# A three-stage kernel in fp32 halves: the last pair's down product by seven products instead of eight

## The chip, the core and the metric

One core of a Trainium2 chip runs the whole program. The metric is the device time of one execution in microseconds, the median of several runs; lower is better. An engine's work is shown by the profiler in time from the first to the last instruction, which is called the span.

## The reference

Chunked attention feeds two feed-forward networks, all in float32, on 4608 tokens of width 512. What the change touches is the first network's last product (`w_out`) and the start of the second network.

```python
x = attention(q, k, v)                   # 8 x 576 tokens, chunks of 64, 8 heads of 64
rms = np.sqrt(np.mean(x * x, axis=-1, keepdims=True) + 1e-06)
xn = x / rms * rms_g
g = xn @ w_gate                          # 512 -> 1536
val = xn @ w_val                         # 512 -> 1536
x = (g / (1 + np.exp(-g)) * val) @ w_out # 1536 -> 512
h = x @ w_in                             # 512 -> 2048
out = (h * np.clip(h + 3.0, 0.0, 6.0) / 6.0) @ w_out2
```

## The kernel before

Tokens are worked in nine blocks of 512, features stand on the partitions. Each fp32 operand is kept as a high and a low half, and a product of two operands is three matmuls (high by high, low by high, high by low). Blocks 0 to 2 of the first network are done plainly. Blocks 3 to 8 are done in three pairs (`for p in range(3)`, L1366). In a pair, the up part (gate and value matrices) is done as a two-by-two block product by seven products (Strassen's method in Winograd's form): the sums of weight blocks (`wo` tiles, loaded from the scratch tensors `ops`) and the sums of token blocks (`xu` tiles) were made earlier, and `product` (L1003 to L1014) issues six matmuls for each of 14 slots. The down part (`w_out`) is not: for each of the two blocks and each of 12 feature groups `mm_down_a` (L1020 to L1031) issues 12 matmuls on weights `wd`, loaded from `keep_out`, and on activations split into halves `gs` by ScalarE and GpSimd (`split_wp`, L1357). `y_store` then moves the four banks out to `yd`.

The second network does block 0 plainly (L1522 to L1554, with `x_fill` beside it, which loads the next pair's activations `x4` from `yd` and makes its sums), and then four pairs in which both the up and the down part go by seven products; there `product_down` (L1584 to L1588) issues six matmuls per step on activation splits that `split_by` (L1578) makes on ScalarE and VectorE four steps ahead.

The order of work is written by hand: each engine executes what the Python code issues, in that order. Side work is placed by ticks: `at(t, fn)` puts a function in an agenda and `tick()` runs it, about every 12 matmuls. In the last pair the side work is `Stash`: it prepares the second network's weights, loads them on ScalarE's DMA queue and stores their sums from that queue. The weight loads (`wo`, `wd`, `wq`) and stores of results go on the SP queue in program order. Weight tiles come from a pool `wp` of 36 buffers of 4 KB per partition; the tiles `q k qT kT p v` of the attention are single buffers, used by the second network's weight loads (`Stream`) later. At the start, while the first tokens are attended, tiny matmuls named `warm0` to `warm3` keep TensorE busy; the digit names the tile whose PSUM bank they write (bank 2i + 1). They stand in the table `START`, an order written out by hand.

## Time and profile before

| what | value |
|---|---|
| median of 3 runs | 1654.99 us (1652.78 to 1657.39) |
| the profiled execution | 1653.22 us |
| its span | 1651.4 us |
| TensorE (PE) busy in the span | 1639.8 us, 99% |
| VectorE (DVE), ScalarE (ACT), GpSimd (POOL) busy | 1036.2, 846.2, 453.7 us |
| granted TensorE clock | 1.0 in every slice (2.4 GHz) |

The profile's page gives for each engine the time in which it executes something. The chain of waits follows, from the last instruction back, what released each step. The wait view lists who waited for whom; the windows view gives busy times in chosen stretches of the span; the timeline lists instructions in order of time. L with a number is a line of the program.

### The profile page before, as it was taken

How to read it: one execution, taken by the hardware profiler on the slowest of the kernel's cores; microseconds unless marked ns; L12 is line 12 of the kernel's file. 1: busy time of each engine (PE TensorE's matmuls, PEld its weight loads, DVE VectorE, ACT ScalarE, POOL GpSimd, SP SyncE). 2: the span in 40 equal slices, each digit the busy share in tenths (PEclk: the TensorE clock that was granted, in tenths of full speed). 3: DMA queues.
4: the chain of work that ended last, by engine and by line, in shares of the span. 5: the costliest groups of instructions: out<-in, count | busy, mean ns of one | idle time of the engine just before them, and what ended most of it. 6: DMA issues, size and time to landing. Idle time of an engine off the chain costs nothing.

```text
span 1651.4 us, 26427 instructions
## 1 busy us (share of the span) xinstructions
PE 1639.8 (99%) x9911; PEld 1348.9 (82%) x9911; DVE 1036.2 (63%) x1534; ACT 846.2 (51%) x1409; POOL 453.7 (27%) x331
## 2 busy tenths in 40 slices
PE   8999999999999999999999999999999999999998
PEld 7888887888888888888888878888888888888887
DVE  7997566655575755748334388358746764875475
ACT  6885445445464455645434344455545544654553
POOL 1002333322236422354226522140024003301310
PEclk9999999999999999999999999999999999999999
DMA  9924677747977698855979675767877796687666
GB/s 295 285 46 112 203 215 208 215 149 234 313 264 241 202 288 281 279 214 209 339 237 330 256 266 199 227 191 249 215 219 218 217 241 199 222 225 232 194 197 161
DMA packets 336097, 375.08 MB, mean 227 GB/s; under 512 B 184288, under 2 KB 260064, under 8 KB 335840
## 3 DMA queue, kind: packets, MB, share of 16 engines
q1 hardware_dynamic: 266080, 302.32, 59.8%
q10 hardware_dynamic: 69888, 71.06, 12.6%
q8 instruction: 79, 1.29, 0.3%
q14 instruction: 50, 0.41, 0.1%
HBM read 292.55 MB, written 80.74 MB: 226 GB/s over the span
## 4 chain that ended last, share of the span: by engine, by line
PE 95%; DVE 2%; DMA 1%; issue 1%; SPq 1%; POOL 0%; ACT 0%; DVEq 0%; POOLq 0%; ACTq 0%
PE PS L1014 39%; PE PS L1588 18%; PE PS L1003 13%; PE PS L1028 6%; PE PS L1029 6%; PE PS L1031 6%; PE PS L908 1%; PE PS L835 1%; DMA wo<-ops 1%; PE PS L817 1%; PE PS L1040 1%; PE PS L1036 1%; PE PS L1790 1%; PE PS L1037 1%; DMA x<-yd 0%
## 5 line engine op out<-in xcount | busy, mean ns | idle before, releaser
L1014 PE MATMUL PS<-xu,wo 128*128 128x512 f32 x1512 | 350.2, 391 | 0.5 <-DVE xu L1230 0.5
L1014 PEld LDWEIGHTS PS<-xu,wo 128*128 128x128 f32 x1512 | 282.0, 188 | 59.8 <-DVE xu L1230 0.9
L1014 PE MATMUL PS<-xo,wq 128*128 128x512 f32 x1344 | 305.3, 389 | 0.0
L1588 PE MATMUL PS<-gs,wq 128*128 128x512 f32 x1296 | 295.3, 389 | 0.0
L1014 PEld LDWEIGHTS PS<-xo,wq 128*128 128x128 f32 x1344 | 252.3, 188 | 52.3
L1588 PEld LDWEIGHTS PS<-gs,wq 128*128 128x128 f32 x1296 | 242.9, 188 | 51.8 <-DVE gs L1582 1.2
L1003 PE MATMUL PS<-XH,w 128*128 128x512 f32 x576 | 146.4, 395 | 1.0 <-DVE w L220 1.0
L1003 PEld LDWEIGHTS PS<-XH,w 128*128 128x128 f32 x576 | 106.2, 188 | 24.9 <-DVE w L220 1.8
L1028 PE MATMUL PS<-gs,wd 128*128 128x512 f32 x288 | 113.2, 393 | 0.0
L1029 PE MATMUL PS<-gs,wd 128*128 128x512 f32 x288 | 112.2, 389 | 0.0
L1059 POOL TENSOR_TENSOR al<-sg,ah 128x512 fp32r<-128x512 f32 x40 | 57.1, 1427 | 153.7 <-ACT ah L1057 152.5
L1360 POOL TENSOR_TENSOR gs<-gu,gs 128x512 fp32r<-128x512 f32 x60 | 84.1, 1421 | 45.7 <-ACT gs L1359 40.1
L1364 DVE TENSOR_TENSOR gu<-gu,PS 128x512 f32<-128x512 f32 x60 | 41.1, 686 | 86.5 <-ACT gu L1446 45.4
L1656 POOL TENSOR_TENSOR gt<-gx 128x512 f32<-128x512 f32 x8 | 10.4, 1294 | 296.5 <-DVE gx L1653 296.5
L1582 DVE TENSOR_TENSOR gs<-gu,gs 128x512 fp32r<-128x512 f32 x88 | 68.0, 792 | 31.7 <-ACT gs L1581 31.5
L1581 ACT CAST gs<-gt 128x512 fp32r<-128x512 f32 x96 | 58.3, 623 | 44.0 <-DVE gt L1725 33.0
L1519 DVE SCALAR_TENSOR_TENSOR gu<-gu,PS 128x512 f32<-128x512 f32 x48 | 32.8, 684 | 72.9 <-ACT gu L1516 72.9
L1003 PE MATMUL PS<-XL,w 128*128 128x512 f32 x288 | 77.3, 390 | 0.0
L1031 PE MATMUL PS<-gs,wd 128*128 128x512 f32 x288 | 77.0, 389 | 0.0
L1057 ACT CAST ah<-sg 128x512 fp32r<-128x512 f32 x52 | 32.4, 624 | 74.9 <-DVE sg L1344 48.5
L1581 ACT CAST gs<-gu 128x512 fp32r<-128x512 f32 x96 | 57.4, 620 | 25.0 <-DVE gs L1582 17.7
L1656 POOL TENSOR_TENSOR gt<-gu 128x512 f32<-128x512 f32 x24 | 32.6, 1359 | 129.0 <-DVE gu L1653 124.8
(249 smaller groups left out, 2833.3 us busy)
## 6 DMA issues: line engine op xcount, KB each, us to landing
wq<-stash_in SPq DMA_DIRECT2D x128, 512.0 KB
wo<-ops SPq DMA_DIRECT2D x126, 512.0 KB
wq<-sums_out SPq DMA_DIRECT2D x64, 512.0 KB
wq<-stash_out SPq DMA_DIRECT2D x48, 512.0 KB
wd<-keep_out SPq DMA_DIRECT2D x36, 512.0 KB
yd<-yst SPq DMA_DIRECT2D x18, 512.0 KB
ops<-w ACTq DMA_DIRECT2D x36, 256.0 KB
v<-in_v_dram SPq DMA_DIRECT2D x32, 256.0 KB
```

Source lines behind the costliest of these rows:

```text
L1003: nc.tensor.matmul(ps, w(wi, c), xs[c][xi], start=(i == 0), stop=(i == n - 1))
L1014: nc.tensor.matmul(PS[:, bank, :], op[:, wi, c * 128:(c + 1) * 128], x[xi][:, c, :], start=first and i == 0, stop=last and i == 5, skip_gr ...
L1028: nc.tensor.matmul(ps, wm[0], a[0], start=first, stop=False)
L1029: nc.tensor.matmul(ps, wm[1], a[0], start=False, stop=False)
L1031: nc.tensor.matmul(PS[:, banks[m], :], w[:, 0, m * 128:(m + 1) * 128], a[1], start=False, stop=last)
L1059: nc.gpsimd.tensor_tensor(lo, t, hi.bitcast(F32), op=ALU.subtract)
L1360: e.tensor_tensor(w[:, 1, :], t, w[:, 0, :].bitcast(F32), op=ALU.subtract)
L1364: nc.vector.tensor_tensor(o, x, y, op=op)
L1581: nc.scalar.copy(w[:, 0, :], x)
L1582: e.tensor_tensor(w[:, 1, :], x, w[:, 0, :].bitcast(F32), op=ALU.subtract)
L1588: nc.tensor.matmul(PS[:, banks[m], :], op[:, wi, m * 128:(m + 1) * 128], x[xi], start=first and (wi, xi) == (0, 0), stop=False, skip_group ...
L1656: nc.gpsimd.tensor_tensor(slot(i, "t"), slot(i, "12"), slot(i, "11"), op=ALU.subtract)
```

## The change

Three things are changed.

1. In the last pair (p == 2) the down part goes by seven products too, with `product_down` and `split_by` as in the second network. It has 42 steps of six matmuls (seven products, six feature groups each) in place of 24 groups of 12. The activations of the up part are laid out anew (`slot`): both token blocks and both features of a group go in tiles `1` and `2`, and GpSimd makes two differences per feature group (`sums_g`); a third is made on VectorE ahead of the step. The results go out as four halves (`kept`, `more`, `y_put`) at the ends of the seven groups of steps.
2. The sums of `w_out` blocks that this needs are made from the kept weights, in the last pair's up part: `OutSums`, six of them, five ticks apart, starting six ticks into the part. Each loads two `keep_out` tiles (SP queue), adds their halves, makes four sums and splits them again (VectorE and ScalarE), and stores four pieces to a new scratch tensor `keep_sums` from ScalarE's queue. Its tiles are the attention's buffers `q`, `k`, `kT`, `p`, used in turn. The down part loads 21 weight tiles (12 of sums, 9 of blocks, the latter in two DMAs each) in place of 12.
3. The second network's plain block uses other PSUM banks (2, 3 for its up product, 4 to 7 for its down product, before 6, 7 and 2 to 5), and asks for its first `x4` tile before its first product instead of after. In `START`, many `warm2` become `warm1`, `warm0` or `warm3`: their count and places stay, their banks change.

The diff, cut to its core (lines of `START` stand for the table; `split_by` and `product_down` are moved up unchanged):

```diff
-    out_q2 total3 total1 share3 share1 scores0 warm2 warm2 warm2 warm2 scores2 trans_p3 top0 less0 top2 less2 Wm0
-    out_p3 expo0 warm2 warm2 warm2 warm2 trans_p1 values3 out_p1 expo2 Wm1 out_x3 square3 total0 Wb0 total2 Wb1
+    out_q2 total3 total1 share3 share1 scores0 warm1 warm1 warm1 warm1 scores2 trans_p3 top0 less0 top2 less2 Wm0
+    out_p3 expo0 warm1 warm1 warm1 warm1 trans_p1 values3 out_p1 expo2 Wm1 out_x3 square3 total0 Wb0 total2 Wb1
...
+    class OutSums:
+        def buf(self, n, kind=F32):
+            return at_p.tile([128, 2, 512], kind, tag=(("q", "k"), ("kT", "p"))[self.i % 2][n], name="os")
...
+            for z, t in enumerate((self.u, self.r)):
+                nc.sync.dma_start(out=t, in_=o1[2 * self.i + z])
...
+            nc.vector.tensor_tensor(self.u[:, z, :], t[:, 0, :], t[:, 1, :], op=ALU.add)
...
+            tt(a22, a21, a22, op=ALU.add)
+            tt(a21, a11, a21, op=ALU.subtract)
+            tt(a11, a22, a11, op=ALU.subtract)
+            tt(a12, a12, a11, op=ALU.subtract)
...
+                nc.scalar.copy(self.h[:, z, :], u)
+                nc.vector.tensor_tensor(u.bitcast(F32R), u, self.h[:, z, :].bitcast(F32), op=ALU.subtract)
...
+                for y, t in enumerate((self.h.bitcast(F32), self.u)):
+                    nc.scalar.dma_start(
+                        out=e1[:, 2 * z:2 * z + 2, self.i, y, :],
...
+                (0, self.load), (4, self.whole, 0), (5, self.whole, 1), (6, self.sums), (7, self.split), (8, self.keep),
...
+        for k_, part in ((O11, 3), (O1, 3), (O2, 3), (O12, 2), (O3, 3), (O12, -1), (O4, 3), (O22, 3)):
+            order += [(2, "out", j, k_) for j in (range(part) if part > 0 else range(3 + part, 3))]
+        for i in range(NI):
+            OutSums(i).plan(P0 + 2 * PAIR + 6 + 5 * i)
...
+                    if p == 2 and i == NI - 1 and pr in (2, 7):
+                        nx.append(split_by(nc.gpsimd, slot(len(nx), "11")))
...
+                        if p == 2:
+                            sums_g(i_)
...
+            for n, (pr, i) in enumerate(steps):
...
+                product_down(bk[z], loads.t[key][:, i % 2], nx.popleft(), pr in (1, 5) and i == 0)
...
+                feed(n + 4)
...
-                for _ in range(1 + 5 * c):
+                for _ in range(6 if c else 2 if b == 1 else 1):
...
+        go(fill, 1)
...
-            bank = 6 + n % 2
+            bank = 2 + n % 2
...
-                mm_down_b(W["out2", fs[n - 1]], prev, n == 1, False, base=2)
+                mm_down_b(W["out2", fs[n - 1]], prev, n == 1, False, base=4)
```

TensorE's order at the last pair, before: the up part (L1014), then the down part, which goes on in the same pattern for 24 groups.

```order
L1014 MATMUL PS<-xu,wo 128x512 x504
L1028 MATMUL PS<-gs,wd 128x512
L1029 MATMUL PS<-gs,wd 128x512
L1028 MATMUL PS<-gs,wd 128x512
L1029 MATMUL PS<-gs,wd 128x512
```

And now, up to the second network's first product (L1062):

```order
L1073 MATMUL PS<-xu,wo 128x512 x504
L1436 MATMUL PS<-gs,wd 128x512 x252
L1062 MATMUL PS<-xr,wq 128x512 x24
L1095 MATMUL PS<-w,ah 128x512
L1096 MATMUL PS<-w,ah 128x512
```

The down part is now one run of 252 matmuls of the same shape, where 24 groups of 12 (288) stood.

The SP queue in the middle of the last pair's up part, before (`wo` from `ops_121` to `ops_123`, the weights of three feature groups; each row is one or more loads):

```order
L461 DMA wo<-ops_121 128x1024 x4
L461 DMA wo<-ops_122 128x1024
L461 DMA wo<-ops_121 128x1024 x2
L461 DMA wo<-ops_122 128x1024 x4
L461 DMA wo<-ops_123 128x1024
```

And now, with the loads `os` of kept weights between them:

```order
L461 DMA os<-keep_out_127 128x1024
L461 DMA os<-keep_out_128 128x1024
L510 DMA wo<-ops_121 128x1024
L510 DMA wo<-ops_122 128x1024
L510 DMA wo<-ops_121 128x1024 x2
L510 DMA wo<-ops_122 128x1024
L461 DMA os<-keep_out_129 128x1024
L461 DMA os<-keep_out_130 128x1024
L510 DMA wo<-ops_122 128x1024 x3
```

A pair of `os` loads stands ahead of every few `wo` loads; it goes into buffers that the stores of the sums before last must have left.

TensorE at the start, with the semaphores that each row waits for, before (transposes of a tile's weights `v` (L570), `warm` matmuls (L638), then the products with the values, L585):

```order
L570 MATMUL PS<-ident,v 128x128 x3
L638 MATMUL PS<-ones_r 128x256 [waits DVE_49]
L638 MATMUL PS<-ones_r 128x256 x3
L570 MATMUL PS<-ident,v 128x128 [waits Pool_49]
L570 MATMUL PS<-ident,v 128x128 x3
```

And now:

```order
L629 MATMUL PS<-ident,v 128x128 x3
L697 MATMUL PS<-ones_r 128x256 x4
L629 MATMUL PS<-ident,v 128x128 [waits Pool_49]
L629 MATMUL PS<-ident,v 128x128 x3
L644 MATMUL PS<-pT,v 64x64 [waits DMAHW1_49,Activation_49]
```

The four `warm` matmuls no longer wait for VectorE at that place.

## Rows read from the trace of the kernel before

**Rows 1.** The page: engines' busy time, then the chain's shares by engine.

```profile
PE 1639.8 (99%) x9911; PEld 1348.9 (82%) x9911; DVE 1036.2 (63%) x1534; ACT 846.2 (51%) x1409; POOL 453.7 (27%) x331
...
PE 95%; DVE 2%; DMA 1%; issue 1%; SPq 1%; POOL 0%; ACT 0%; DVEq 0%; POOLq 0%; ACTq 0%
```

**Rows 2.** TensorE's waits over the span: total us, times, longest.

```profile
PE PS L638 <- DVE v L550: 1.8, 1, 1.8
...
PE PS L1036 <- ACT ah L1057: 0.6, 1, 0.6
PE PS L1014 <- DVE xu L1230: 0.5, 1, 0.5
```

**Rows 3.** The chain of waits: start us, us, what ran.

```profile
767.48 114.24 PE PS L1014 x504
...
1111.89 76.49 PE PS L1588 x336
```

**Rows 4.** The same chain at the changeover to the second network.

```profile
946.10 0.91 PE PS L1031 x4
947.00 2.73 PE PS L1003 x12
```

**Rows 5.** Timeline of the start, TensorE: start, us, operation, idle before it.

```profile
16.24 0.74 PE L638 MATMUL PS<-ones_r 128*128 128x256 f32 x4 [1.80 <-DVE v L550]
...
35.79 1.21 PE L1003 MATMUL PS<-XH,w 128*128 128x512 f32 x4 [0.79 <-DVE w L220]
```

**Rows 6.** The same stretch, VectorE.

```profile
16.10 0.68 DVE L558 TENSOR_REDUCE sm<-v 128x8 f32<-128x512 f32 x1
...
27.61 0.16 DVE L622 RECIPROCAL r<-r 128x1 f32<-128x1 f32 x1 [0.24 <-ACT r L615]
...
28.47 0.16 DVE L622 RECIPROCAL r<-r 128x1 f32<-128x1 f32 x1 [0.30 <-ACT r L615]
...
30.69 0.29 DVE L624 TENSOR_SCALAR pT<-ident,r 128x128 f32<-128x128 f32 x1 [0.53 <-PE PS L638]
```

**Rows 7.** Timeline of the changeover: the `x4` load, its use, TensorE.

```profile
952.96 0.57 SPq L1491 DMA_DIRECT2D x<-yd  x1
...
961.22 0.69 DVE L1499 TENSOR_TENSOR xt<-x 128x512 f32<-128x512 f32 x1 [2.26 <-issue]
...
963.94 0.50 PE L1036 MATMUL PS<-w,ah 128*128 128x512 f32 x1 [0.62 <-ACT ah L1057]
```

**Rows 8.** Windows: PE, PEld, DVE, ACT, POOL busy, clock, DMA share, GB/s.

```profile
776.00:832.00 56.00, 56.00 (x249) 46.37 (x248) 21.28 (x34) 24.90 (x42) 14.66 (x11) 1.00 0.97 351
924.00:940.00 16.00, 16.00 (x72) 13.27 (x71) 6.65 (x5) 7.21 (x13) 13.35 (x10) 1.00 1.03 410
767.50:881.70 114.20, 114.20 (x505) 94.56 (x505) 50.44 (x78) 52.60 (x91) 30.11 (x22) 1.00 0.84 292
881.70:947.00 65.30, 65.30 (x290) 54.07 (x289) 24.06 (x22) 21.53 (x40) 44.38 (x32) 1.00 0.80 294
...
1111.90:1188.40 76.50, 76.50 (x337) 62.95 (x337) 65.75 (x100) 43.20 (x77) 6.22 (x4) 1.00 0.81 239
```

**Rows 9.** DMA of the last pair, 767.5 to 947 us: bytes, then issues.

```profile
DMA packets 22203, 52.58 MB, mean 293 GB/s; under 512 B 1840, under 2 KB 12080, under 8 KB 22064
...
wo<-ops SPq DMA_DIRECT2D x36, 512.0 KB
w<-stash_out SPq DMA_DIRECT2D x14, 512.0 KB
wd<-keep_out SPq DMA_DIRECT2D x12, 512.0 KB
```

**Rows 10.** Second network's down part, groups: busy us, mean ns, idle before.

```profile
L1582 DVE TENSOR_TENSOR gs<-gu,gs 128x512 fp32r<-128x512 f32 x22 | 17.2, 793 | 8.1 <-ACT gs L1581 8.0
L1582 DVE TENSOR_TENSOR gs<-gt,gs 128x512 fp32r<-128x512 f32 x24 | 16.1, 685 | 0.2 <-ACT gs L1581 0.2
...
L1725 DVE TENSOR_TENSOR gt<-gu,gt 128x512 f32<-128x512 f32 x12 | 8.2, 684 | 0.0
```

**Rows 11.** Who waited in the last pair, 767.5 to 947 us: total us, times, longest.

```profile
ACT s L1451 <- DMA stash_in<-sc: 1.0, 1, 1.0
```

**Rows 12.** A weight load that ended a stretch of the chain: start, us.

```profile
350.82 7.29 DMA wo<-ops
```

**Rows 13.** VectorE's sums of the same form beside and without GpSimd: min/median/max ns.

```profile
L376 DVE TENSOR_TENSOR ou<-ou x8: 410/412/1398, 952.4 to 1029.2; 128x256 f32<-128x256 f32 x8
...
L384 DVE TENSOR_TENSOR oh<-ou,oh x16: 677/1020/1372, 957.0 to 1034.3; 128x512 fp32r<-128x512 f32 x16
...
L372 DVE TENSOR_TENSOR ou<-w x16: 678/684/686, 951.1 to 1026.9; 128x512 f32<-128x512 f32 x16
```

More of the change, by code (lines that the diff above doesn't have):

```diff
@@ L464, in ahead @@
                     )
+                elif p_ == 2:
+                    t = wp.tile([128, 2, 2, 256], F32R, tag="w", name="wd")
+                    if k_ < 4:
+                        nc.sync.dma_start(out=t.bitcast(F32), in_=e1[:, k_, 2 * i:2 * i + 2])
+                    else:
+                        z, h = divmod(k_ - 4, 2)
+                        for n in range(2):
+                            nc.sync.dma_start(
+                                out=t.bitcast(F32)[:, n], in_=o1[4 * i + z + 2 * n][:, :, h * 256:(h + 1) * 256]
+                            )
                 else:
@@ L1285, in fused_kernel @@
         A11, S2_, S1_, S3_, A12, S4_, A21, A22 = range(8)
-        O2, O3, O4, O1, O11, O21, O12, O22 = range(8)
         NG = NQ // 2
@@ L1361, in split_wp, with split_by, product_down @@
             return w[:, 0, :], w[:, 1, :]
+        def split_by(e, x):
+            w = wp.tile([128, 2, N], F32R, tag="w", name="gs")
+            nc.scalar.copy(w[:, 0, :], x)
+            e.tensor_tensor(w[:, 1, :], x, w[:, 0, :].bitcast(F32), op=ALU.subtract)
+            return w[:, 0, :], w[:, 1, :]
+        def product_down(banks, op, x, first):
+            for wi, xi in ((0, 0), (1, 0), (0, 1)):
+                for m in range(2):
+                    nc.tensor.matmul(
+                        PS[:, banks[m], :],
+                        op[:, wi, m * 128:(m + 1) * 128],
+                        x[xi],
+                        start=first and (wi, xi) == (0, 0),
+                        stop=False,
+                        skip_group_check=True,
+                    )
         def vec(o, x, y, op):
@@ L1384, in fused_kernel @@
             items = [(z, f) for z in range(2) for f in range(FA)]
-            hold, later = {}, None
+            hold, later, nx = {}, None, deque()
             for i in range(NI + 1):
@@ new lines, in fused_kernel, with feed @@
+            steps = [
+                (pr, i)
+                for pr, span in (
+                    (1, range(NI)), (5, range(NI)), (6, range(NI)), (2, range(4)), (7, range(NI)),
+                    (2, range(4, NI)), (3, range(NI)), (4, range(NI)),
+                )
+                for i in span
+            ]
+            def feed(n):
+                if n + 2 < len(steps) and steps[n + 2][0] in (6, 4):
+                    pr, i = steps[n + 2]
+                    t = slot(i, "t")
+                    vec(t, slot(i, "22" if pr == 6 else "21"), t, ALU.subtract)
+                if n < len(steps):
+                    pr, i = steps[n]
+                    x = slot(i, {1: "11", 5: "t", 6: "t", 2: "21", 7: "12", 3: "22", 4: "t"}[pr])
+                    nx.append(split_by(nc.vector, x))
@@ L1577, in slot @@
             return G[key]
-        def split_by(e, x):
-            w = wp.tile([128, 2, N], F32R, tag="w", name="gs")
-            nc.scalar.copy(w[:, 0, :], x)
-            e.tensor_tensor(w[:, 1, :], x, w[:, 0, :].bitcast(F32), op=ALU.subtract)
-            return w[:, 0, :], w[:, 1, :]
-        def product_down(banks, op, x, first):
-            for wi, xi in ((0, 0), (1, 0), (0, 1)):
-                for m in range(2):
-                    nc.tensor.matmul(
-                        PS[:, banks[m], :],
-                        op[:, wi, m * 128:(m + 1) * 128],
-                        x[xi],
-                        start=first and (wi, xi) == (0, 0),
-                        stop=False,
-                        skip_group_check=True,
-                    )
         def bank(z, m):
```

143 lines of the change are left out of this document (112 added, 31 removed).

## The prediction

> **What bounds the kernel now.** I read the page first: TensorE is busy 99% of the span and carries 95% of the chain [rows 1]. The reader should see that this leaves 1651.4 - 1639.8 = 11.6 us in which TensorE is idle at all; no other engine is busy for more than 63%. Then the chain in order of time: in the last pair it is one run of 504 matmuls in 114.24 us, 0.2267 us each, and the second network's down part, which already has the form that the last pair is to get, is a run of 336 in 76.49 us, 0.2277 us each [rows 3]. So a matmul of this shape costs 0.227 us of time wherever the operands are there; the 389 ns or so that a timeline shows for one is its length in a pipeline. Third, TensorE's waits: the few that exist are at the start and at the changeover to the second network [rows 2]; in the last pair there is none. Last the windows of the last pair, for what else is close to full: VectorE 50 of 114 us and 24 of 65, GpSimd 44 of 65 in the down part, and the DMA engines, 0.84 and 0.80 of the time [rows 8]. The DMA engines are the one resource to which the change adds much and which has little left.
>
> **The change part by part.** The profiled execution took 1653.22 us, of which 1651.4 are span; it lies 1.77 us under the median of 1654.99. I make the sum as a difference and put it on both.
>
> *Matmuls.* The down part falls from 24 x 12 = 288 to 42 x 6 = 252 matmuls. 36 x 0.227 = 8.2 us, all of it on the path, since TensorE goes without a wait from the pair's first to its last matmul. Nothing hides it and nothing new is put on TensorE. **-8.2.**
>
> *Start.* The four `warm` matmuls waited 1.80 us for VectorE's subtraction on the tile whose bank they share [rows 5]; in the new order they don't. What is late next is VectorE itself: from 16.10 us until it releases the first products at 35.79 it works without a pause but for 0.24, 0.30 and 0.53 us, each a wait for something that TensorE gave late [rows 6]. So at most 1.07 us of the 1.80 comes through; bounds 0 and 1.07, and I take 0.9, as TensorE and ScalarE both run more than a microsecond earlier by then. After 35.79 TensorE is full and keeps the gain. **-0.9.**
>
> *Changeover.* The load of `x4` was issued at 952.96, six microseconds after the last product of the pair ended at 947.0, VectorE waited 2.26 us for it at 961.22, and TensorE 0.62 us behind that [rows 4, 7]. Now it is asked for ahead of the first product, and only the last result half has to leave before it on the SP queue. The bounds are 0 and 0.62; I take 0.6. The other banks cost nothing: 2 and 3 are read out long before the pair's end, and 6 and 7, which are read out last, are written only from the second feature group on, 24 matmuls or 5.4 us after. **-0.6.**
>
> *Sums of kept weights.* On VectorE, 12 additions of 0.684 us, 24 quarter sums of 0.41 and 12 subtractions of about 1.0 [rows 13] are 30 us more in the up part: 50 becomes 81 of 114. ScalarE gets 12 casts, some 7 us, on 53, and 24 issues of stores. GpSimd gets 12 differences of about 1.4 us, 17 on 30. None becomes full, and the cover is the matmuls. VectorE stands in front of TensorE where it empties a bank: there it has two slots of six matmuls, 2.7 us, less its own 0.69. A wait of VectorE for an `os` load, or a burst of four sums at the slow 1.4 us (row L376, beside GpSimd), can exceed that by 1 to 3 us. Bounds 0 and 6 for the six pieces together. The nearest rows are ScalarE's wait of 1.0 us for a transfer in the up part, behind which TensorE did not wait [rows 11, 2]: I take 0.
>
> *VectorE in the down part.* It takes over 38 splits (0.69 to 0.79 us), makes 12 differences of 0.684 [rows 10] and four additions to results, 37 to 41 us. What stays of its 24 us is some 22, measured while GpSimd was busy 44 of 65 us and some operations took up to three times their usual time, as in rows 13; GpSimd now sheds 24 splits, so I take 10 to 22. The sum is 47 to 63 us in 57.2. The nearest row is the second network's down part, where VectorE is busy 65.75 of 76.50 and TensorE does not wait [rows 8, 2]; 86% of 57.2 is 49. I take 0.5 us of loss; bounds 0 and 6. **+0.5.**
>
> *Transfers.* Before, 52.58 MB moved in the last pair [rows 9]. Added are 12 `os` loads of 0.52 MB and 24 stores of 0.26, 12.6 MB, and 21 instead of 12 `wd` loads, 4.7 MB. Of the 69.9 MB some 4.7 (four `wq`, four `w`, two late stores) are asked for behind the second network's first operand, so 65.2 MB must pass before that network can begin. The time for it, from the first load of the pair at about 769.7 to the new end of the down part at 767.5 + 756 x 0.2267 = 938.9, is 169.2 us: 385 GB/s. What can the engines move? 410 GB/s over 16 us in the down part, and 351 over 56 us in the up part, with the share at 0.97 [rows 8]; the latter holds pauses in which the queue had nothing to issue. At 410 the 65.2 MB take 159.0 us and nothing is lost; at 351, 185.8 us, a loss of 16.6. I take the middle, 380 GB/s, since both pauses and full stretches will occur: 171.4 us. **+2.2**, bounds 0 and 16.6. The stalls from VectorE and from transfers overlap, so I don't add their upper ends.
>
> The Trainium skill, page "DMA: Bandwidth & Descriptors", section "Specifications", gives a limit of about 358 GB/s of memory per core. The trace disagrees: 410 GB/s over 16 us [rows 8]. By the page's limit 65.2 MB would take 182.1 us, a loss of 12.9 instead of 2.2.
>
> The sum is -8.2 - 0.9 - 0.6 + 0.5 + 2.2 = -7.0 us: 1646.2 for an execution like the profiled one, and 1654.99 - 7.0 = 1648.0 for the median.
>
> **The rivals.**
>
> *The queues run in step (same).* The `os` buffers are two sets, so a pair of `os` loads waits until the stores of the sums before last have landed, and the `wo` loads behind it on the SP queue wait too; the stores in turn are issued by ScalarE behind its own casts, and while ScalarE waits to issue one it empties no bank. Four pairs of loads are held in this way. A weight load takes up to 7.29 us to land [rows 12], and behind the last held pair the order leaves 32 matmuls, 7.3 us, before the first `wo` is needed; so each hold may leave 1 to 1.5 us uncovered, 4 to 6 in all. For it: the DMA is fuller than before, and landing times will be longer. Against it: in the trace the queue runs ahead, and TensorE has no wait in the last pair at all [rows 2]. With 5 us more lost, 1653.0.
>
> *VectorE becomes the bound of the down part (same).* At the upper end of its sum TensorE waits 6 us for splits instead of 0.5: 1648.0 + 5.5 = 1653.5. For it: the 22 us at the slow durations. Against: GpSimd, whose work makes them slow, is relieved.
>
> *The transfers decide (slower).* If the mix with many 1 KB pieces moves no more than the 351 GB/s of the up part's stretch, the second network's first weights land 185.8 us after the pair's loads began, TensorE stands 16.6 us in the last pair, and the whole is 1655.0 - 9.7 + 16.6 = 1661.9. The mechanism decides from 65.2 MB / (169.2 + 9.7) = 364 GB/s downward. For it: the share was 0.97 in that stretch. Against: 410 was reached, with stores and loads mixed, when the queue had enough issued. By the limit in the Trainium skill ("DMA: Bandwidth & Descriptors", "Specifications") the transfers would take 182.1 us and the end would be 1655.0 - 9.7 + 12.9 = 1658.2, no change that can be told; with 410 GB/s in the trace against it, I give that rule 0.02, which lies within the 0.04 below.
>
> *The change doesn't do what it says.* The 36 matmuls are gone from the order, so only the start and the changeover can fail: 1649.5.
>
> **How the numbers follow.** A measurement of this kernel can tell 0.3%, about 5 us, from no change: faster means under 1650.0, slower over 1660.0. I give my forecast, with its neighbourhood from 1644.5 to 1650 (there the failed start or changeover lies too), 0.70; queues in step or VectorE as the bound, 1650 to 1656, 0.19; transfers at 354 to 364 GB/s, 1656 to 1660, 0.04; transfers at 351 or less, over 1660, 0.07. So faster 0.70, same 0.23, slower 0.07. The range reaches down to a change without any loss and the whole of the start's gain, 1655.0 - 8.2 - 1.1 - 0.6 = 1645.1, less half a microsecond of spread, and up to the queues' case with 7 us lost more than I take, 1655.0.
>
> **What would show it.** In the profile after, the chain should have a run of 252 matmuls of `product_down` on `wd` at 0.227 each, and TensorE's busy time should be down by 8. The wait of `warm` for VectorE of 1.8 us should be gone, and the first products should begin near 34.9. The last pair should take 172 to 175 us from its first `wo` product to the second network's first product, with the DMA share there over 0.9 and some 390 GB/s. If instead TensorE waits in the up part behind ScalarE or VectorE, or for `wo` loads, the queues run in step; waits for `gs` in the down part would show VectorE; a wait for `wq` or `wd` at the end, with the share at 1, the transfers. The forecast would be wrong above all if the added 17 MB find no room, which is its least certain term.

## The result and the profile after

The changed kernel takes 1666.76 us (median of five runs, 1662.83 to 1671.8), the kernel before beside it 1653.59 us (1652.37 to 1657.39). The ratio is 1.007, 95% interval 1.0056 to 1.0085: slower, and over the 1660.0 that the prediction set for it, where 1648.0 and a range of 1644.5 to 1655.0 were forecast. The profiled execution, the fastest of the five, took 1662.83 us with a span of 1661.0; the 4 us between it and the median are in no trace.

The page, as [rows 1] for before: the engines' busy times, then the chain's shares by engine.

```profile
PE 1639.9 (99%) x9875; PEld 1343.1 (81%) x9875; DVE 1100.8 (66%) x1631; ACT 863.9 (52%) x1445; POOL 449.1 (27%) x324
...
PE 87%; DMA 6%; DVE 4%; issue 1%; ACT 1%; POOL 0%; ACTq 0%; SPq 0%; DVEq 0%; POOLq 0%
```

TensorE has 36 matmuls fewer and is as long busy as before, and the DMA, which carried 1% of the chain, carries 6%. TensorE's waits, as [rows 2] for before: total us, times, longest.

```profile
PE PS L1095 <- ACT ah L1116: 2.5, 1, 2.5
PE PS L1073 <- DVE gu L1446: 1.9, 1, 1.9
PE PS L1073 <- ACT gu L1552: 1.7, 1, 1.7
PE PS L687 <- DVE pT L683: 1.4, 2, 0.7
PE PS L1073 <- DMA wo<-ops: 1.3, 1, 1.3
PE PS L697 <- DVE ones_r L1148: 1.2, 1, 1.2
PE PS L1436 <- ACT gs L1429: 1.2, 1, 1.2
PE PS L1436 <- DVE gs L1430: 1.0, 3, 0.5
```

Lines L1073 and L1436 are the up products and the last pair's down products, L1095 is the second network's first block, L687 and L697 belong to the start. Before, the second network's block had one wait of 0.6 us, the up products one of 0.5, and the down products none [rows 2].

To see where the time went I cut the run at four matmuls that exist in both kernels: the first of the last pair, the first of its down part, the first of the second network, and the first regular up product of the second network's pairs. "Lost" is the time between the starts of neighbouring matmuls beyond 0.227 us, summed over the steps longer than 0.24 us; it holds waits and lower clock alike.

| | before | after |
|---|---|---|
| first matmul of the last pair at | 767.32 | 767.21 |
| lost in the up part (504 matmuls) | 0 | 8.7 |
| lost in the down part (288, now 252) | 0 | 7.2 |
| lost at the changeover | 1.6 | 3.2 |
| the three together, from the first cut to the last | 268.25 | 278.02 |
| from the last cut to the last matmul | 611.93 | 611.93 |

All of the difference lies in this stretch, called the stage from here on: 19.1 us lost there instead of 1.6, against 8.2 saved; half a microsecond more is in steps shorter than 0.24 us.

Windows of after, as [rows 8] for before: busy times of PE, PEld, DVE, ACT and POOL, clock, DMA share, GB/s; the whole of the two parts first, then pieces.

```profile
795.00:965.00 170.00, 161.51 (x680) 127.88 (x679) 125.87 (x179) 78.90 (x143) 63.48 (x43) 0.98 1.00 362
767.40:890.60 123.20, 117.70 (x505) 95.00 (x505) 83.63 (x123) 56.24 (x101) 49.58 (x35) 0.99 0.98 353
890.60:955.00 64.40, 61.41 (x253) 47.43 (x253) 53.59 (x74) 34.90 (x64) 20.97 (x13) 0.97 0.98 359
...
950.00:965.00 15.00, 15.00 (x62) 11.93 (x61) 8.69 (x15) 5.06 (x9) 2.95 (x3) 0.92 1.03 416
```

The DMA engines are full for 170 us on end (share 1.00) and move 362 GB/s; in the same 170 us the kernel before had a share of 0.81 at 285 GB/s. In the up part their rate is 353, in the last 15 us 416. Over the two parts they moved 66.6 MB in 187.7 us, 355 GB/s.

How that reaches TensorE is seen at 869 to 884 us. From the timelines of ScalarE with its DMA queue (ACTq), of VectorE and of TensorE: start, us, instruction, and in brackets the idle time before it and what ended it.

```profile
868.78 4.18 ACTq L485 DMA_DIRECT2D keep_sums<-os  x4
...
879.24 0.37 ACTq L288 DMA_DIRECT2D stash_out<-slo  x1
...
881.56 0.62 ACT L1429 CAST gs<-ge 128x512 fp32r<-128x512 f32 x1 [1.27 <-DMA keep_sums<-os]
883.08 0.59 ACT L1552 COPY gu<-PS 128x512 f32<-128x512 f32 x1
...
883.70 0.69 DVE L1446 TENSOR_TENSOR gu<-gu,PS 128x512 f32<-128x512 f32 x1 [10.23 <-ACT gu L1552]
...
883.72 3.06 PE L1073 MATMUL PS<-xu,wo 128*128 128x512 f32 x12 [1.72 <-ACT gu L1552]
```

Four stores of sums take ScalarE's queue 4.2 us to issue, and the second of the next two stores leaves 3.5 us after the first (875.73 and 879.24), because issues wait here until earlier transfers have landed; a store of sums takes up to 9.9 us to land (869.25 to 879.16). ScalarE executes in order, so the copy that empties a bank (L1552) comes late, VectorE stands 10.23 us for it, and TensorE 1.72 us behind both.

Which transfer an issue waits for is read from the semaphores of the trace. A transfer reports its landing by counting up a semaphore. The 1312 loads and stores that SP and ScalarE issue share eight of them, 164 each, and 1151 of the issues wait for their own, that is until the transfer that had it before has landed. So about eight of these transfers are under way at a time, and an issue on one queue can stand behind a transfer of the other: the first of the four stores above waited for an `os` load (landed at 868.76), the third for a `wo` load (871.91), both of the SP queue. In the up part 13 of ScalarE's issues were held in this way by more than 0.15 us, 16.9 us in all; in the kernel before, none.

A stall can cost twice. TensorE's clock by the windows view of TensorE (busy, granted clock, DMA share, GB/s):

```profile
819.00:820.00 1.00, 1.00 (x6) 1.00 1.01 414
...
823.00:824.00 1.00, 1.00 (x4) 0.50 0.92 264
824.00:825.00 1.00, 1.00 (x4) 0.50 0.97 359
```

After the 1.9 us wait for VectorE that ended at 822.46 the granted clock is 0.50 (1.2 GHz) up to 826, and again from 949.0 to 952.4 behind three waits of 0.25, 1.25 and 0.32 us between 945 and 949. Each of the two costs 1.7 us: 3.4 of the 19.1.

### The profile page after: what moved, and what is told of

It reads as the page before. It is cut to its first block, busy times and chain, and to the rows that moved or that the text cites. A ratio compares the mean times of both kernels' runs of the same rounds, so it can differ in the third digit from the quotient of the medians.

```text
span 1661.0 us, 26625 instructions
## 1 busy us (share of the span) xinstructions
PE 1639.9 (99%) x9875; PEld 1343.1 (81%) x9875; DVE 1100.8 (66%) x1631; ACT 863.9 (52%) x1445; POOL 449.1 (27%) x324
## 4 chain that ended last, share of the span: by engine, by line
PE 87%; DMA 6%; DVE 4%; issue 1%; ACT 1%; POOL 0%; ACTq 0%; SPq 0%; DVEq 0%; POOLq 0%
PE PS L1073 35%; PE PS L1436 19%; PE PS L1062 13%; PE PS L1087 5%; PE PS L1088 4%; PE PS L1090 4%; DMA w<-stash_out 2%; DMA keep_sums<-os 1%; PE PS L967 1%; PE PS L894 1%; PE PS L876 1%; PE PS L1095 1%; PE PS L1096 1%; PE PS L1099 1%; PE PS L1944 1%
## 5 line engine op out<-in xcount | busy, mean ns | idle before, releaser
L1073 PE MATMUL PS<-xu,wo 128*128 128x512 f32 x1512 | 353.7, 393 | 6.0 <-DVE gu L1446 1.9
L1073 PEld LDWEIGHTS PS<-xu,wo 128*128 128x128 f32 x1512 | 282.4, 188 | 68.4 <-DVE gu L1446 2.4
L1073 PE MATMUL PS<-xo,wq 128*128 128x512 f32 x1344 | 305.3, 389 | 0.0
L1436 PE MATMUL PS<-gs,wq 128*128 128x512 f32 x1296 | 295.3, 389 | 0.0
L1073 PEld LDWEIGHTS PS<-xo,wq 128*128 128x128 f32 x1344 | 252.3, 188 | 52.3
L1436 PEld LDWEIGHTS PS<-gs,wq 128*128 128x128 f32 x1296 | 243.0, 188 | 51.7 <-DVE gs L1430 1.2
L1062 PE MATMUL PS<-XH,w 128*128 128x512 f32 x576 | 146.3, 395 | 1.0 <-DVE w L220 0.9
L1062 PEld LDWEIGHTS PS<-XH,w 128*128 128x128 f32 x576 | 106.2, 188 | 24.7 <-DVE w L220 1.8
L1430 DVE TENSOR_TENSOR gs<-gu,gs 128x512 fp32r<-128x512 f32 x121 | 96.3, 817 | 38.9 <-ACT gs L1429 38.5
L1429 ACT CAST gs<-gu 128x512 fp32r<-128x512 f32 x130 | 77.5, 621 | 46.8 <-DVE gs L1430 19.3
L1062 PE MATMUL PS<-XL,w 128*128 128x512 f32 x288 | 77.2, 390 | 0.0
L1087 PE MATMUL PS<-gs,wd 128*128 128x512 f32 x192 | 75.9, 395 | 0.0
L1088 PE MATMUL PS<-gs,wd 128*128 128x512 f32 x192 | 74.8, 390 | 0.0
L266 POOL TENSOR_TENSOR slo<-sraw,sc 128x512 fp32r<-128x512 f32 x32 | 48.7, 1521 | 87.8 <-ACT sc L265 73.9
L1807 DVE SCALAR_TENSOR_TENSOR gu<-r,gu 128x512 f32<-128x512 f32 x48 | 42.2, 880 | 36.5 <-ACT r L1687 36.0
```

The source lines that it names most:

```text
L266: nc.gpsimd.tensor_tensor(lo, x, hi.bitcast(F32), op=ALU.subtract)
L1062: nc.tensor.matmul(ps, w(wi, c), xs[c][xi], start=(i == 0), stop=(i == n - 1))
L1073: nc.tensor.matmul(PS[:, bank, :], op[:, wi, c * 128:(c + 1) * 128], x[xi][:, c, :], start=first and i == 0, stop=last and i == 5, skip_gr ...
L1087: nc.tensor.matmul(ps, wm[0], a[0], start=first, stop=False)
L1088: nc.tensor.matmul(ps, wm[1], a[0], start=False, stop=False)
L1429: nc.scalar.copy(w[:, 0, :], x)
```

## The experiments

All stage numbers are of one profiled execution each. Where a run left out work, its text says which. Stretches at half clock as in after are in the stage of most of these profiles too, and half their length, at most, counts in the losses: 1.7 us in e2, e3, e4, e5, e7, e9 and e13, 3.4 in e15 and e17, 5.1 in e6 and e10, 8.5 in e11, none in e8, e12, e14 and e16.

| run | up | down | changeover | stage | median us | its kernel before |
|---|---|---|---|---|---|---|
| before | 0 | 0 | 1.6 | 268.3 | 1653.6 | |
| after | 8.7 | 7.2 | 3.2 | 278.0 | 1666.8 | 1653.6 |
| e2 no sums | 0 | 7.0 | 1.2 | 266.8 | 1653.3 | 1653.2 |
| e3 sums without transfers | 0.6 | 3.7 | 5.5 | 268.3 | 1653.8 | 1653.2 |
| e4 sums without arithmetic | 8.2 | 6.5 | 3.1 | 276.7 | 1662.7 | 1653.2 |
| e5 sums early | 0 | 4.9 | 4.4 | 267.8 | 1663.6 | 1653.2 |
| e7 sums in pairs 0 and 1 | 0 | 7.4 | 0.6 | 266.6 | 1661.2 | 1654.5 |
| e6 no sums, fetches early | 0 | 13.8 | 0 | 272.3 | 1654.5 | 1654.5 |
| e8 as e7, fetches early | 0 | 7.7 | 0 | 266.3 | 1659.9 | 1654.5 |
| e9, e17 sums' stores on SP | 4.8, 6.1 | 5.3, 7.3 | 2.3, 1.0 | 271.1, 273.1 | 1657.8 (one time), 1658.2 | 1654.5, 1653.8 |
| e10 no sums, stash on GpSimd | 2.4 | 12.8 | 2.0 | 275.9 | 1665.1 | 1653.8 |
| e11 sums' stores and stash on GpSimd | 19.3 | 10.0 | 6.9 | 295.2 | 1681.6 | 1653.8 |
| e12 no sums, six loads less | 0 | 2.2 | 0.2 | 260.9 | 1647.0 | 1653.8 |
| e15 no sums, stash on SP | 0 | 4.0 | 7.3 | 269.9 | 1654.7 | 1653.9 |
| e13 whole sums | 2.8 | 10.0 | 0.9 | 272.4 | 1660.8 | 1653.9 |
| e14 whole sums, stores on SP | 0.8 | 9.9 | 0.8 | 270.4 | 1656.7 | 1653.9 |
| e16 the same, stash on SP too | 0.5 | 8.6 | 1.7 | 269.5 | 1657.3 | 1653.9 |

**The sums: transfers or arithmetic.** The theory is that the sums' 12.6 MB of transfers fill the DMA; the rivals are their arithmetic, and the down part itself. Three runs take the sums apart.

```diff
-        for i in range(NI):
-            OutSums(i).plan(P0 + 2 * PAIR + 6 + 5 * i)
...
-                        nc.sync.dma_start(out=t.bitcast(F32), in_=e1[:, k_, 2 * i:2 * i + 2])
+                        nc.sync.dma_start(out=..., in_=o1[4 * i + k_]...)
```

> The sums of kept weights are left out (their loads, their arithmetic on VectorE and ScalarE, their stores); the loads of `wd` that would read the sums read as many bytes of the kept blocks, so the result is not the reference's. The stage is measured from the first matmul of the last pair to the first regular up product of the second network: 268.2 us before, 278.0 after, 259.3 if the 36 matmuls were all that changed. Theory 1 (the sums' 12.6 MB of transfers fill the DMA, and the issues on ScalarE then wait for landings): the loss of 18.7 us is nearly gone, stage 260 to 263, time 1645 to 1648. Rival 2 (the sums' arithmetic on VectorE): the same here. Rival 3 (the down part itself, its splits on VectorE and its 21 weight loads): 4 to 9 us stay lost, all of them after the last up product, stage 264 to 269, time 1650 to 1655.

Without sums the up part loses nothing, but the time, 1653.31 us, is that of the kernel before (ratio 1.0005, 0.9995 to 1.0014): 7.0 us stay lost in the down part. Theory 1 holds for the up part only, and rival 3 for the rest.

```diff
-                nc.sync.dma_start(out=t, in_=o1[2 * self.i + z])
+                nc.gpsimd.memset(t, 0.0)
...
-                ... (7, self.split), (8, self.keep),
+                ... (7, self.split),
```

> The sums' arithmetic stays, on buffers that GpSimd fills with zeros; their loads and stores are left out, and `wd` reads as many bytes of the kept blocks; the result is not the reference's. Theory 1 (transfers): as without any sums, stage 260 to 264, time 1645 to 1649. Rival 2 (arithmetic on VectorE and ScalarE): most of the 18.7 us stay, stage 272 to 278, time 1658 to 1664. Rival 3 (down part): stage 264 to 269.

```diff
-                (0, self.load), (4, self.whole, 0), (5, self.whole, 1), (6, self.sums), (7, self.split), (8, self.keep),
+                (0, self.load), (8, self.keep),
```

> The sums' loads and stores stay, with the loaded tiles stored as they are; their arithmetic is left out, and the result is not the reference's. Theory 1 (transfers): most of the 18.7 us stay, stage 272 to 278, time 1657 to 1665. Rival 2 (arithmetic): stage 260 to 264, time 1645 to 1649. Rival 3 (down part): stage 264 to 269 with the up part without loss.

The arithmetic alone costs 0.6 us in the up part, the transfers alone 8.2 of after's 8.7; the times agree, 1653.80 and 1662.70 (ratios 1.0007 and 1.006). VectorE had in the first of these

```profile
767.40:882.00 114.60, 114.25 (x504) 94.31 (x503) 88.88 (x123) 59.27 (x104) 62.46 (x48) 1.00 0.82 291
```

88.9 of 114.6 us to do (the third busy time), and TensorE did not feel it. In the second it is the DMA that is full, as in after:

```profile
795.00:890.00 95.00, 89.23 (x384) 72.48 (x383) 35.03 (x47) 35.61 (x63) 37.90 (x30) 0.98 0.99 361
```

**The sums elsewhere.** Two runs make them where the DMA has room.

```diff
-            return at_p.tile([128, 2, 512], kind, tag=(("q", "k"), ("kT", "p"))[self.i % 2][n], name="os")
+            return st_p.tile([128, 2, 512], kind, tag="st", name="os")
...
-                nc.sync.dma_start(out=t, in_=o1[2 * self.i + z])
+            t = W["out", 2 * self.i + z].bitcast(F32)
...
-            OutSums(i).plan(P0 + 2 * PAIR + 6 + 5 * i)
+            OutSums(i).plan((3, 10, 17, 41, 51, 61)[i])
```

> The sums are made some 200 to 600 us earlier, in the second and third block, from the weights that still lie in the on-chip memory (no loads), in two buffers that the blocks' results use; 6.3 MB of stores leave there, where the DMA share is 0.4 to 0.75. The result is the reference's. Theory 1 and rival 2 alike: the last pair is as without sums, stage 260 to 263; the blocks take the 30 us of VectorE (busy 155 of 246 us there) beside the matmuls at a cost of 0 to 2 us; time 1645 to 1650, below the kernel before. Rival 3 (down part): 1650 to 1656.

The up part came out as without sums, but the last pair began at 777.87 instead of 767.21: 10.7 us were lost in the blocks, where 0 to 2 were expected. TensorE's waits in 36 to 778 us are for engines that came late:

```profile
PE PS L873 <- POOL p L867: 3.1, 1, 3.1
PE PS L1059 <- DVE sg L1405: 1.8, 1, 1.8
PE PS L1059 <- ACT sg L1401: 1.5, 1, 1.5
PE PS L835 <- DVE kT L816: 1.1, 1, 1.1
```

The sums gave GpSimd no work. In the longest of these waits GpSimd had itself stood 2.85 us for VectorE, which had split sums just before:

```profile
199.50 2.37 DVE L477 TENSOR_TENSOR os<-os 128x512 fp32r<-128x512 f32 x2
...
203.58 2.23 POOL L867 TENSOR_TENSOR p<-p,rs 128x1024 f32<-128x1024 f32 x1 [2.85 <-DVE rs L862]
```

With that wait the granted clock fell to 0.50, from 205.2 to 212.0, which is some 3 of the 10.7 us.

```diff
-            OutSums(i).plan(P0 + 2 * PAIR + 6 + 5 * i)
+            OutSums(i).plan(P0 + i // 3 * PAIR + (8, 24, 43)[i % 3])
```

> The changed kernel with the six pieces of sums moved to the first two pairs, three in each, in the two buffers of the result stores; the result is the reference's. If the up part's loss of 8.7 us is a matter of crowding in one pair, it is gone and the first two pairs lose 0 to 2 us (DMA share there 0.8): the last pair's first matmul at 767 to 770, the stage 266 to 268 as without sums, time 1652 to 1656. If each piece costs wherever it stands, the last pair starts 6 to 9 us later and the time is 1659 to 1663.

Again the last pair is as without sums and the place pays: it begins at 775.74, 8.5 us late. There the waits are for the attention's transposes behind VectorE (`kT`, 3.5 us in four waits), for `gu` (2.0) and for `wo` loads (1.4).

**Who issues the stores.** The same bytes, issued from SP instead of ScalarE.

```diff
-                    nc.scalar.dma_start(
+                    nc.sync.dma_start(
                         out=e1[:, 2 * z:2 * z + 2, self.i, y, :],
```

> The changed kernel with the 24 stores of the sums issued from the SP queue instead of ScalarE's; the same bytes. If the up part loses its 8.7 us because ScalarE stands at the issues of these stores, the loss falls to 0 to 4 us. If it is the bytes, the loss stays at 7 to 10 us, with TensorE waiting for `wo` loads instead. If the SP queue, held by stores whose data isn't ready, falls behind, the loss grows over 10 us.

> The changed kernel with the 24 stores of the sums issued from the SP queue, timed. If ScalarE's holds at these issues are a part of the up part's 8.7 us, the median is 1656 to 1661 (1666.8 with the stores on ScalarE's queue) and the up part loses 3 to 6 us; if the one look was luck, the median is 1663 to 1668 and the loss 7 to 10.

The timed run gave 1658.18 us (1655.13 to 1661.6; ratio 1.0024, 1.0014 to 1.0033), 8.6 less than after, with 4.8 and 6.1 us lost in the up part in the two profiles. ScalarE's issues were held for 4.5 and 2.8 us there, against 16.9. So a part of the up part's loss was ScalarE standing at issues, and more than half of it stayed with the same bytes, then partly as waits for `wo` (2.3 and 1.8 us).

**The down part: bunched, held, or too many bytes.** In the run without sums ScalarE stood 4.93 and 5.48 us behind issues, and TensorE 2.1 us behind the second. ScalarE's timeline, with the idle time before each in brackets:

```profile
918.02 1.14 ACT L1430 CAST gs<-gu 128x512 fp32r<-128x512 f32 x2 [4.93 <-DMA stash_in<-shi]
...
926.97 0.62 ACT L1430 CAST gs<-gu 128x512 fp32r<-128x512 f32 x1 [5.48 <-DMA w<-stash_out]
...
927.64 3.68 PE L1437 MATMUL PS<-gs,wd 128*128 128x512 f32 x8 [2.12 <-ACT gs L1430]
```

The cast does not read `w`: the transfer that ended the wait belongs to the SP queue, and it was the store's issue ahead of the cast that had waited for it, as they use the same semaphore. So the transfers may be bunched too late in the part; or ScalarE's holds at its issues cost the time (theory A); or the transfers are too many for this stretch, whoever issues them (theory D). First, the fetches of the second network's weights were asked for earlier.

```diff
-                if 7 < j < 22:
-                    stash[(j - 8) // 2].fetch_out(j % 2)
+                if 1 < j < 16:
+                    stash[(j - 2) // 2].fetch_out(j % 2)
```

> Without the sums of kept weights, as the run without sums (the result is not the reference's), and the 14 fetches of the second network's out weights start in the third instead of the ninth twenty-fourth of the down part. Theory (the loss of 7.0 us in the down part without sums comes from transfers bunched in its second half: DMA share 1.0 at 360 to 423 GB/s from 912 to 965 us, 0.8 at 234 to 277 from 882 to 902; ScalarE then stands at its issues): the loss in the down part falls to 0 to 3 us, the stage to 260 to 264 us, the time to 1645 to 1650. Rival (the splits on VectorE, busy 9.8 of 10 us at 882 to 902): the loss stays at 5 to 8 us, stage 265 to 268, time 1650 to 1655.

1654.48 us against 1654.54 before, without sums as in e2: nothing gained. In its profile, of an execution 5 us above the median, the changeover was free of loss, but the down part lost 13.8, with one wait of 4.3 us for ScalarE's cast. The same fetches with the sums in pairs 0 and 1:

> Both: sums in the first two pairs, fetches of the second network's out weights six twenty-fourths earlier; the result is the reference's. If both theories hold, the stage is 260 to 264 us and the time 1645 to 1650, below the kernel before (1653.2); if the splits on VectorE bound the down part, 1651 to 1656.

1659.85 us, 1.0037 of before, with 7.7 lost in the down part. Moving the transfers within the part doesn't help. Next the issues were moved off ScalarE, first to GpSimd.

```diff
-                nc.scalar.dma_start(out=self.d[:, at, self.m, z, :], ...
+                (nc.gpsimd if clock[0] >= P0 + 2 * PAIR else nc.scalar).dma_start(out=self.d[:, at, self.m, z, :], ...
```

> Without the sums of kept weights, as the run without sums (the result is not the reference's), and in the last pair the loads and stores of the stash work are issued by GpSimd instead of ScalarE; the same bytes. There ScalarE stood 5.2 and 5.5 us at such issues, each behind an earlier transfer that took 9 to 14 us to land, and TensorE waited 2.3 us behind the second. Theory A (ScalarE, in order, held at its issues): the down part's loss of 7.0 us falls to 0 to 3, the stage to 260 to 263 us, the time to 1646 to 1649. Theory D (the transfers are too many for 882 to 965 us, whoever issues them): the loss stays at 5 to 8 us, the time at 1652 to 1655, with waits for `wd` or `w` in place of those for casts.

> The changed kernel with the stores of the sums and, in the last pair, the loads and stores of the stash work issued by GpSimd; the result is the reference's. Theory A: the up part's loss falls from 8.7 to 0 to 4 us and the down part's from 7.2 to 0 to 4; stage 261 to 268; time 1646 to 1654. Theory D: stage 272 to 280, time 1657 to 1667.

Both were slower, 1665.05 (no sums) and 1681.62 us, and don't tell the two theories apart: issuing on GpSimd has its own cost, which I had not priced. TensorE's waits in the last pair of the first are now mostly for subtractions on VectorE and GpSimd, around 890 and 898 us, with a DMA share of 0.61 in 882 to 902 us (0.80 without sums):

```profile
PE PS L1437 <- DVE gs L1431: 4.2, 2, 3.4
PE PS L1437 <- POOL gs L1431: 2.5, 1, 2.5
```

The timelines show one thing that stands before the longer of these waits. An operation of VectorE that never takes over 1.51 us in the run without sums took 5.57 us, and ended just after an unbroken row of four operations on GpSimd:

```profile
888.80 5.57 DVE L249 TENSOR_SCALAR sc<-sc 128x512 f32<-128x512 f32 x1 [4.69 <-issue]
...
889.09 1.28 POOL L1431 TENSOR_TENSOR gs<-gu,gs 128x512 fp32r<-128x512 f32 x1
...
892.78 1.30 POOL L266 TENSOR_TENSOR slo<-sraw,sc 128x512 fp32r<-128x512 f32 x1
```

So the test was made again with the SP queue.

> Without the sums of kept weights, as the run without sums (the result is not the reference's), and in the last pair the loads and stores of the stash work are issued by the SP queue instead of ScalarE's; the same bytes, and no work of GpSimd. Theory A (ScalarE held at its issues): the down part's loss of 7.0 us falls to 0 to 3, stage 260 to 263, time 1646 to 1649. Theory D (the bytes): 5 to 8 us, stage 265 to 268, time 1651 to 1655, with waits for `wd` or `w`.

TensorE's waits for ScalarE's casts are gone, and others stand in their place: 2.2 us for `wq` loads and 3.4 for `ah` at the changeover, behind `x4`. Its window from 912 to 962 us:

```profile
912.00:962.00 50.00, 45.32 (x195) 35.90 (x193) 32.45 (x47) 20.64 (x37) 11.35 (x7) 1.00 1.03 403
```

The DMA is full at 403 GB/s whoever issues, and the time, 1654.65, is about that of the run without sums (1653.31): theory D. The loss moved, from 7.0 us in the down part to 4.0, and from 1.2 at the changeover to 7.3; the stage, 269.9, lies above what either theory expected. The direct test takes bytes away.

```diff
-                    if k_ < 4:
+                    if k_ in (2, 7):
+                        nc.gpsimd.memset(t.bitcast(F32), 0.0)
+                    elif k_ < 4:
```

> Without the sums, and six of the 21 `wd` loads (3.1 MB, 8 us of the full DMA) replaced by GpSimd filling the tiles with zeros; the result is not the reference's. Theory D: the down part's loss of 7.0 us falls to 0 to 3, time 1646 to 1650. Theory A: the holds of ScalarE come earlier in the part and stay; loss 4 to 7, time 1650 to 1654.

1646.99 us, 0.9958 of before (0.9942 to 0.9975). Six weight tiles less (nine transfers, 3.1 MB), and 5.9 us of the stage are gone, up to 1.7 of them the half clock of e2; TensorE has one kind of wait left in the last pair:

```profile
PE PS L1439 <- DVE gs L1433: 1.7, 2, 0.9
```

So theory D holds for the down part and the changeover, though fewer bytes are also fewer transfers, which this run does not separate. A is not its opposite: with the bytes the holds went too, from 12.2 us at four of ScalarE's issues in the down part of the run without sums to 3.1 at one. With the sums and these bytes left out, the kernel comes out near the 1648.0 that were forecast for the whole.

**Fewer bytes, nothing left out.** The sums are stored and loaded whole, and split where they are used.

```diff
-                (6, self.sums), (7, self.split), (8, self.keep),
+                (6, self.sums), (7, self.keep),
...
+                        nc.scalar.copy(t[:, :, 0, :], t.bitcast(F32)[:, :, 1, :])
+                        nc.gpsimd.tensor_tensor(
+                            t[:, :, 1, :], t.bitcast(F32)[:, :, 1, :], t.bitcast(F32)[:, :, 0, :], op=ALU.subtract
+                        )
```

> The changed kernel with the sums of kept weights stored and loaded whole instead of as high and low parts: 12 stores of 0.26 MB instead of 24, and 12 `wd` loads of 0.26 MB instead of 0.52, 6.3 MB less in all, half of it in the down part; the high and low parts are made there, by 12 casts on ScalarE and 12 subtractions on GpSimd. The result is the reference's. Bytes as the cause: the up part's loss falls from 8.7 to 3 to 5 us, the down part's from 7.2 to 1 to 4, stage 264 to 270, time 1650 to 1656. ScalarE's holds as the cause: half of its issues for the sums are gone, but 8 us of casts come into the down part, where its holds are: up 3 to 5, down 7 to 10, stage 270 to 276.

> As the run with whole sums, and its 12 stores issued from the SP queue. The result is the reference's. If bytes and issuer add as they did one by one (half of the up part's loss each): up part's loss 0 to 3 us, down part's 1 to 4, stage 261 to 267, time 1646 to 1653. If SP's own holds cost as much: as with ScalarE's queue, stage 264 to 270.

> Whole sums, and in the last pair all of ScalarE's loads and stores, those of the sums and of the stash work, from the SP queue. The result is the reference's. Theory A: up part's loss 0 to 2, down part's 0 to 2, stage 260 to 264, time 1645 to 1650, below the kernel before. Theory D: as whole sums with the sums' stores alone on SP, stage 261 to 267. If SP falls behind the up part, `wo` loads come late and the loss grows to 5 or more there.

1660.80, 1656.66 and 1657.29 us. The up part's loss fell as expected, to 2.8, 0.8 and 0.5 us. But the down part lost 8.6 to 10 us, where 1 to 4 were expected (7 to 10 only in the first run's rival): there the engines are now the bound. The window of the second of these, and that of the run without sums:

```profile
882.00:950.00 68.00, 60.37 (x257) 47.13 (x256) 65.01 (x73) 39.92 (x73) 39.44 (x24) 1.00 0.86 294
```

```profile
882.00:947.00 65.00, 60.40 (x257) 48.82 (x256) 52.40 (x73) 32.74 (x59) 19.77 (x11) 0.97 0.93 336
```

As many instructions of VectorE (73) take 65.0 us instead of 52.4, beside 20 us more of GpSimd's, and fill 96% of the window; TensorE waits for `gs` and for the new splits (3.8 and 3.1 us in the second run). No version that leaves nothing out came out below the kernel before.

**The small parts alone.** The kernel before with only the new banks of the start and of the second network and the early request of `x4`.

> The kernel before with only the new bank order of the start, the second network's banks and the earlier request of `x4`; the result is the reference's. The prediction's terms: first products 0.9 us earlier than 35.79, and the 0.62 us wait at the changeover gone, so that the stage from the last pair's first matmul falls from 268.25 to 267.6 us; time some 1.5 us shorter, 1652. The profile of the whole change had its first products at 35.63 only; if that holds here, the start gives 0.2.

The wait at the changeover is gone (lost there: 0.75 instead of 1.6, stage 267.38 instead of 268.25), at 1653.76 us (one time, beside 1653.76 of the kernel before). At the start nothing came: the first full run of products began at 35.98 us (35.79 before [rows 5]).

## Why the prediction was wrong

The forecast was 7.0 us below before; after is 13.2 above. Point by point:

The last pair took 187.7 us up to the second network's first product, where 172 to 175 were to show it right.

*Matmuls, -8.2.* Right. 36 fewer, in one run of 252, at 0.227 us wherever nothing is missing.

*Transfers, +2.2.* The step that failed. The bytes were right: 65.2 MB were counted, 66.6 moved in the two parts. The rate was not. The text took 380 GB/s, the middle between 410 over 16 us and 351 over 56 us [rows 8], because the latter "holds pauses". It had a share of 0.97: it held hardly any. Over the two parts the rate was 355 GB/s, over the 170 us in which the DMA of after is full 362. By the text's own division 65.2 MB at 355 take 183.7 us, a loss of 14.5 instead of 2.2; the two parts lost 15.9. The right number stood in the row that was averaged away. A full share is not one rate: by the packet records of the 170 us a piece of 1 KB took 47 ns (19,990 of them), which for 16 engines is 348 GB/s, and one of 4 KB 159 ns in the median, 411 GB/s, but 175 in the mean (9,728), 375 GB/s, since 6% of them took longer than 170, up to 2 us. In the row of 410 GB/s they took 160 in the mean. So the many 1 KB pieces (stores of sums and of the stash, half blocks) are a part of it: with every 4 KB piece at 159 ns these pieces would have moved some 385 GB/s (an estimate). The rest is the slow 4 KB pieces, and what slowed them is not shown.

The rival that priced this was the transfers deciding: at 351 GB/s a loss of 16.6 us and 1661.9, deciding from 364 downward, with 0.07 for over 1660 and 0.04 for 354 to 364 GB/s. The measured rate lies in the second band, the time in the first: 1662.8 for the profiled run and 1666.8 for the median. Of its signs the full share came, but no wait for `wd` or `wq` at the end: TensorE's waits were those of the other rival, in the up part for ScalarE, VectorE and `wo` loads.

The limit of about 358 GB/s per core, which the Trainium skill states ("DMA: Bandwidth & Descriptors", "Specifications"), had been set aside because 16 us showed 410. It agrees with the mean over this pair, 353 to 362 GB/s, and not with stretches of it (416 over 15 us); no run shows that it is what sets the mean. By it the forecast, an estimate from the page's figure, would have been 1658.2, nearer, but still 8.6 us short.

*Sums of kept weights, 0 (bounds 0 to 6).* Wrong: 8.7 us, above the upper bound. The arithmetic was judged rightly (0.6 alone). What was missed is that the 24 stores and 12 loads don't only use the DMA: they make every issue wait longer (16.9 us of holds at ScalarE's issues), and ScalarE's issues stand in the same order as the copies that empty TensorE's banks. The rival "the queues run in step" described this, with 4 to 6 us, and put it down to the two sets of `os` buffers; what held ScalarE's issues was the eight shared semaphores. Moving the stores to SP took away 2.6 to 3.9 of the 8.7. This rival and the transfers' were taken as alternatives; here both happened together. How the rest divides between bytes and the holds of the other issues is not settled: the two feed each other.

*VectorE in the down part, +0.5.* Within its bounds: in after TensorE waited 1.0 us for VectorE's splits in three waits, and the run with six weight tiles less lost 2.2 us in the part. VectorE was busy 53.6 us, inside the 47 to 63. It is near its limit, though, as the whole sums showed.

*Start, -0.9.* Not there. The 1.8 us wait for `v` is gone, as said, but the first products began at 35.63 instead of 35.79 [rows 5], and the last pair 0.1 us earlier. VectorE's idle times of 0.24 and 0.30 us [rows 6] have gone, yet TensorE now waits elsewhere for VectorE (`pT`, 1.4 us in two waits), and the third idle time stays:

```profile
30.56 0.29 DVE L683 TENSOR_SCALAR pT<-ident,r 128x128 f32<-128x128 f32 x1 [0.54 <-PE PS L697]
```

The text read all three idle times as waits for something that TensorE gave late; two were ended by ScalarE [rows 6]. The row behind the bound, an idle VectorE, told what could be saved at most; a wait that VectorE itself ends later was counted as saved.

*Changeover, -0.6.* Right alone (0.85 less lost) and lost in the whole, 3.2 instead of 1.6. `x4` was asked for earlier in the order, but the SP queue was by then behind TensorE. From the timelines of SP, VectorE and TensorE, as [rows 7]:

```profile
958.70 0.52 SPq L1662 DMA_DIRECT2D x<-yd  x1
...
971.26 0.69 DVE L1670 TENSOR_TENSOR xt<-x 128x512 f32<-128x512 f32 x1 [3.82 <-issue]
...
973.98 0.50 PE L1095 MATMUL PS<-w,ah 128*128 128x512 f32 x1 [2.54 <-ACT ah L1116]
```

It left at 958.70, 3.8 us after the second network's first product, ahead of which it stands in the order, when a `wq` load on the same semaphore had landed (958.63): an earlier place in a queue that is behind is no earlier time.

## What to carry to other kernels

When a change adds transfers, divide the bytes by the rate that the trace shows at a full share over a long stretch with a like mix of pieces; do not average it with the best short stretch. Where an engine that computes also issues DMAs, look which semaphore each issue waits for and price the issue at the landing time of a full DMA, since everything behind it in the engine's order waits too. And before the same work is moved to a quieter place, ask which engine is close to its limit there: the sums cost 8 to 11 us in each of the three places where they were made.

## What the runs showed of the hardware

- An issue on one queue can be held by a transfer of another, where the program gives both the same semaphore: in the run without sums ScalarE's cast stood 5.48 us behind stores whose issues waited for the landing of SP's loads, which neither store nor cast reads.
- Loads and stores issued by GpSimd made the kernel 12 us slower than the same issued by ScalarE (1665.05 against 1653.31 us without sums). VectorE's operation of 5.57 us beside GpSimd's unbroken row (at most 1.51 us in the run without sums) is one place of it. How the 12 us divide is not shown.
- The Trainium skill ("SBUF — State Buffer", "SBUF: two separate sides") says that DMAs issued by GpSimd get their descriptors from GpSimd's cores, which VectorE locks out while it runs an operation in a two-port mode. The DMA share, 0.61 where it was 0.80, would fit, but no run here shows that lock.
- A wait of TensorE of about 2 us was followed by a granted clock of 0.50 for 3.4 us, 1.7 us lost, in after (1.9 us, ended at 822.46) and without sums (2.1 us, ended at 927.64). So were three shorter waits close together (1.8 us in all, 945 to 949). The 2.5 us wait that ended at 973.98 was not.
- With the DMA at a full share, 4 KB pieces took 159 ns in the median everywhere, but 160 in the mean over the 16 us at 410 GB/s before, and 175 over the 170 us at 362.
